# GpSimd's elementwise steps as one instruction each instead of two to four pieces, in an attention and feed-forward kernel

## The chip, the cores and the metric

The kernel runs on one core of one Trainium2 chip. The metric is device time in microseconds of one execution; the profile is one further execution with the hardware profiler on. Engines are named as the profile names them: PE is TensorE, DVE is VectorE, ACT is ScalarE, POOL is GpSimd, SP is SyncE (here the queue that issues the DMAs).

## What is computed

Four batches of eight heads, 768 rows, head width 64. Each row of Q and K gets a bucket from the signs of six projections; a score counts only where the buckets agree. After the softmax and the product with V, the heads of a row are joined to 512 numbers, which go through a feed-forward layer of width 2048 with the exact GELU.

```python
q_bits = (np.einsum('bhsd,dk->bhsk', q, proj) > 0)
k_bits = (np.einsum('bhsd,dk->bhsk', k, proj) > 0)
mask = q_bucket[:, :, :, None] == k_bucket[:, :, None, :]
scores = np.where(mask, scale * np.matmul(q, k.transpose(0, 1, 3, 2)), -1e9)
attn = exp(scores - max); attn = attn / (sum(attn) + 1e-09)
x = (attn @ v).transpose(0, 2, 1, 3).reshape(B * S, H * D)
h = x @ w_in
out = (0.5 * h * (1.0 + erf(h / sqrt(2)))) @ w_out
```

## The kernel before

**Numbers in two halves.** Most float32 products are made of float16 parts: a value is scaled by a power of two, rounded to a high half, and the rest becomes a low half. That takes a scaling (`affine`, one tensor input) and either one VectorE instruction of two SBUF inputs (scale and subtract in one) or, on GpSimd, a scaling in place and a subtraction (`subtract`, two tensor inputs). Such splits are made of Q and K of 24 heads (`head`, `add_low` at L625 on), of the two weight matrices (`weight_pair`), of V (`values_halves`) and of the attention weights (`unit`, `high` and `low` at L984 on). The first batch's heads keep plain float32 (`head_plain`), and the attention weights of some units are divided in place and turned by TensorE (`whole_turn`, L1031).

**A row block.** 32 heads of six blocks of 128 rows give 192 units. A unit is: scores on TensorE into one of two PSUM buffers `s` (L952 for plain heads, L954 and L955 for split ones); the row maxima on VectorE (L958, `rows<-s`); one or two 128x1 steps on GpSimd, VectorE or ScalarE (L963 and L438, `rows<-rows`); the exponential on ScalarE (L972), which sets the `s` buffer free for the next scores; a reciprocal (L981); the high half of the attention weights (L438 or L434, into `hl`, or into `wraw`, which serves as more of the same buffers after the weights are read); the low half on VectorE (L987); a DMA that transposes both halves (L994); and the product with V (L1084).

**A head** of the later batches: load (`raw`), largest value (L603), scale, high half `Q`, copies of it by DMA or an engine (`K<-Q`), the two low halves of Q and K (on GpSimd: `raw<-raw,hs` at L438 and `K<-raw,Q` at L459), the projections onto the six bits on TensorE (L668), their signs on ScalarE (L674), and the mask rows (`Q<-sign`).

**The feed-forward part** runs for 256 rows at a time: L1300 (hidden layer), L1310 (ScalarE takes it out of PSUM), L1338 (GELU), the high and low halves of the result (`g`, L438 and L1352) and L1382 (second product), L1412 (VectorE takes it out). TensorE works it in between the attention's units, and alone after the last of them.

**What sets the order.** A planner (`Plan.order`) plays all steps through with estimated costs and fixes each step's engine and each engine's order; the instructions are then written out in that order, and every engine works through its own in order, waiting on semaphores. The costs are numbers in `affine_cost`, `subtract_cost` and in the `on` tables of steps (2.8 for a low half on GpSimd). They hold for a step, however it is issued.

**The lines that the change touches.** `pieces` (L422) cuts a GpSimd step's tiles along the free dimension: an `affine` into pieces of at most 512 columns, a `subtract` into pieces of at most 256. So 768 columns are two pieces of 384 or three of 256, and 1,024 columns two of 512 or four of 256. Steps on VectorE and ScalarE are never cut, and GpSimd's steps of 512 columns or fewer in `affine` (`g`, the mask rows, the 128x1 steps) are one piece already.

Of the kernel before, what the change touches and what calls it, by code (L numbers as in the profile page):

```python
# [16 lines left out]
ALU = mybir.AluOpType  # L17
# [235 lines left out]
def tile_bucket_attention_moe(  # L253
# [94 lines left out]
    def buf(step):  # L348
# [32 lines left out]
        out=praw[:, NBIT:], in0=praw[:, :NBIT], scalar1=-1.0, scalar2=None, op0=ALU.mult  # L381
# [37 lines left out]
            top = add("DVE", 0.07, emit, key, [top], port=emit is inverse)  # L419
        return top  # L420

    def pieces(engine, most, *aps):  # L422

        whole, n = aps[0].shape[1], 1
        for size in aps[0].shape[1:]:
            n *= size
        count = -(-n // most) if engine == "Pool" else 1
        cuts = [whole * k // count for k in range(count + 1)]
        return [tuple(x[:, i:j] for x in aps) for i, j in zip(cuts, cuts[1:])]

    def affine(engine, out, in_, scale=1.0, bias=0.0):

        if engine == "ACT":
            nc.scalar.activation(out=out, in_=in_, func=AF.Copy, scale=scale, bias=bias)  # L434
        else:
            on = nc.vector if engine == "DVE" else nc.gpsimd
            for o, x in pieces(engine, 512, out, in_):
                on.tensor_scalar(out=o, in0=x, scalar1=scale, scalar2=bias, op0=ALU.mult, op1=ALU.add)  # L438

    def affine_cost(engine, n, pointer=False):  # L440
        base, rate, extra = {
# [13 lines left out]

    def subtract(engine, out, in0, in1):
        on = nc.vector if engine == "DVE" else nc.gpsimd
        for o, x, y in pieces(engine, 256, out, in0, in1):
            on.tensor_tensor(out=o, in0=x, in1=y, op=ALU.subtract)  # L459

    def subtract_cost(engine, n):
        return 0.14 + 1.042e-3 * n if engine == "DVE" else 0.2 + 2.2e-3 * n
# [4 lines left out]
    def everywhere(t, top, key):  # L467


        def diagonal():  # L470
            affine(dg.engine, buf(dg), ident, t[:, 0:1])

        def spread():
            nc.tensor.matmul(buf(pm)[:, :P], ones, buf(dg), start=True, stop=True)

        def biggest():
            nc.vector.tensor_reduce(out=t[:, 1:2], in_=buf(pm)[:, :P], axis=AX.X, op=ALU.max)

        dg = add(affine_on("DI", P, True), 0, diagonal, key, [top], takes="diag", port=True)
        pm = add("PE", 0.11, spread, key, [dg], takes="hp")  # L480
        free(dg, [pm])
        sc = add("DVE", 0.2, biggest, key, [pm])
        free(pm, [sc])
        return sc
# [105 lines left out]
    def head(b, h, i, key, clear, cl):  # L590
# [16 lines left out]
        def high():  # L607
            affine(hi.engine, aq, buf(raw), sc)

        def add_move(dst, src, rd, rs):  # L610
            box = []

            def move():
                out, in_ = sets[i][dst][rd], sets[i][src][rs]
                if box[0].engine == "SP":
                    nc.sync.dma_start(out=out, in_=in_)
                else:
                    affine(box[0].engine, out, in_)

            on = {  # L620
                "DVE": (0.27, PAR["NM_DVE"]), "ACT": (0.84, PAR["NM_ACT"]), "Pool": (0.9, PAR["NM_Pool"]),
                "SP": (0.45, PAR["NM_SP"]),
            }
            box.append(add(on, 0, move, key + PAR[f"DUP{cl}"], [hi], port=True))
            return box[0]  # L625

        def add_low(dst, rd, rs):
            box = []

            def low():  # L630
                out, a = sets[i][dst][rd], aq[rs]
                x = buf(raw)[rs]
                if box[0].engine == "DVE":
                    nc.vector.scalar_tensor_tensor(
                        out=out, in0=x, scalar=sc[rs], in1=a, op0=ALU.mult, op1=ALU.subtract
                    )
                else:
                    affine("Pool", x, x, sc[rs])
                    subtract("Pool", out, x, a)

            on = {"DVE": (1.04, PAR["NL_DVE"]), "Pool": (2.8, PAR["NL_Pool"])}
            box.append(add(on, 0, low, key + PAR[f"LOW{cl}"], [hi], port=True))
            return box[0]
# [57 lines left out]
    def weight_pair(name, srcs, dsts, inv, key, step):  # L701
# [76 lines left out]
        for f, dst in zip(fs, dsts):  # L778
            box = []

            def scaled(f=f, box=box):
                affine(
                    box[0].engine, buf(box[0]).rearrange("p (c f) -> p c f", c=n), f.bitcast(F32), t[:, 2:3]
                )

            def high(dst=dst, box=box):
                affine(box[1].engine, dst[:, 0], buf(box[0]).rearrange("p (c f) -> p c f", c=n))

            def low(dst=dst, box=box):
                subtract(  # L790
                    box[2].engine, dst[:, 1], buf(box[0]).rearrange("p (c f) -> p c f", c=n), dst[:, 0]
                )

            ws = add(affine_on("WS", 1024, True), 0, scaled, key + PAR["P" + name], [sc], takes="o", port=True)
            hi = add(affine_on("WH", 1024), 0, high, key + PAR["P" + name], [ws], port=True)
            lo = add(subtract_on("WL", 1024), 0, low, key + PAR["Q" + name], [hi], port=True)
            box += [ws, hi, lo]
            los.append(lo)
            splits[name][-1].append(ws)
            free(ws, [lo])  # L800
# [346 lines left out]
    whole = tuple((c, TC) for c in range(0, S, TC))  # L1147
# [26 lines left out]
    for n_pass, (b, chunks) in enumerate(passes):  # L1174
# [7 lines left out]
        for pos, h in enumerate(heads):  # L1182
            pr = h // 2
            if pos % 2 == 0:
                key, mms = t - PAR[f"V{cl}"], []
                whole = pos // 2 < WHOLE[n_pass]
# [6 lines left out]
            i = next((i for i in range(n_sets) if owner.get(i, ())[:2] == (b, h)), None)  # L1193
            kept = i is not None
            if not kept:
                i = min(range(n_sets), key=lambda i: (used.get(i, -1), i))
# [277 lines left out]
```

## Time and profile before

| | us |
|---|---|
| median of three runs | 916.1 (915.82 to 916.74) |
| the profiled execution | 916.96 |
| its span, first to last instruction | 915.1 |
| TensorE busy | 865.3 |
| VectorE busy | 677.9 |
| ScalarE busy | 648.7 |
| GpSimd busy | 484.9 in 745 instructions |

The profile is read as busy time of each engine, in the whole span and in stretches; as waits, each an idle time of an engine with the instruction that ended it; as groups of instructions with their durations; and as instructions in order of time. A duration on GpSimd or VectorE runs from the instruction's start to its end, so what it waits for with its operands ready, inside the instruction, makes it longer.

### The profile page before, as it was taken

What the parts mean: (1) busy time and instruction counts of PE and PEld (TensorE: products, weight loads), DVE (VectorE), ACT (ScalarE), POOL (GpSimd) and SP (SyncE); (2) the same over time, 40 slices, a digit from 0 to 9 for tenths busy, and PEclk for the clock granted to TensorE, in tenths of its full rate; (3) what the DMA queues carried; (4) which work ended last, traced back from release to release, by engine and by line L of the source; (5) the groups of instructions that cost most, each with busy time, mean ns of one, the idle gap of its engine ahead of it and who ended that gap; (6) DMA issues with size and microseconds to landing.
All of it is one profiled execution on the core that took longest, in us unless ns stands there. A gap on an engine that the chain in (4) does not pass through costs nothing. (4 is left out here: it accounts for less than half of the span.)

```text
span 915.1 us, 18464 instructions
## 1 busy us (share of the span) xinstructions
PE 865.3 (95%) x6893; PEld 574.4 (63%) x6893; DVE 677.9 (74%) x1441; ACT 648.7 (71%) x1090; POOL 484.9 (53%) x745
## 2 busy tenths in 40 slices
PE   8998999988999989999889999999999999999998
PEld 5665556654755746656647656656666667676763
DVE  5999997987997998888889988987878761212122
ACT  3798889987878787888888797887767653232221
POOL 2486769587758677776877477675723310000000
PEclk9999999999999999999999999999999999999999
DMA  9963362316777888776888876876775750000000
GB/s 256 248 181 111 92 188 70 93 31 122 166 159 149 152 184 172 139 151 151 132 166 172 184 167 139 162 142 127 116 122 116 127 117 1 24 2 24 1 24 24
DMA packets 282394, 112.17 MB, mean 123 GB/s; under 512 B 228800, under 2 KB 269888, under 8 KB 282304
## 3 DMA queue, kind: packets, MB, share of 16 engines
q1 hardware_dynamic: 282000, 110.98, 56.0%
q8 instruction: 54, 0.88, 0.4%
q14 instruction: 36, 0.29, 0.1%
q10 hardware_dynamic: 304, 0.00, 0.0%
HBM read 43.13 MB, written 6.29 MB: 54 GB/s over the span
## 5 line engine op out<-in xcount | busy, mean ns | idle before, releaser
L1300 PE MATMUL hp<-x,Win 128*128 128x256 f16 x2304 | 267.1, 273 | 2.8 <-DVE x L1112 2.4
L1382 PE MATMUL hp<-Wout,g 128*128 128x512 f16 x1152 | 261.6, 379 | 0.0
L1300 PEld LDWEIGHTS <-Win 128*128 128x128 f16 x2304 | 225.2, 98 | 42.4 <-issue 6.4
L1382 PEld LDWEIGHTS <-g 128*128 128x128 f16 x1152 | 109.9, 98 | 126.3 <-issue 4.4
L958 DVE TENSOR_REDUCE rows<-s 128x1 f32<-128x768 f32 x192 | 178.8, 945 | 7.4 <-PE s L955 5.7
L972 ACT ACTIVATE p<-s,rows 128x768 f32<-128x768 f32 x142 | 140.3, 988 | 22.4 <-POOL rows L438 10.5
L1310 ACT ACTIVATE h<-hp,ffs 128x512 f32<-128x512 f32 x96 | 65.5, 682 | 101.3 <-PE hp L1300 100.8
L954 PE MATMUL s<-Q 88*128 88x384 f16 x304 | 99.5, 327 | 13.9 <-ACT p L972 8.6
L955 PE MATMUL s<-K 128*128 128x384 f16 x304 | 99.4, 327 | 0.0
L459 POOL TENSOR_TENSOR K<-raw,Q 64x256 f16<-64x256 f32 x120 | 93.5, 805 | 3.2
L438 DVE TENSOR_SCALAR g<-h,ffs 128x512 f16<-128x512 f32 x30 | 15.0, 500 | 107.4 <-ACT h L1338 77.3
L1084 PE MATMUL hp<-pt,vhl 128*64 128x256 f16 x1296 | 77.6, 274 | 4.8 <-DVE o L1412 2.3
L987 DVE SCALAR_TENSOR_TENSOR hl<-p,rows,hl 128x768 f16<-128x768 f32 x66 | 72.2, 1096 | 13.4 <-POOL hl L438 11.2
L1084 PEld LDWEIGHTS <-vhl 128*64 128x64 f16 x1296 | 69.3, 110 | 14.6 <-issue 13.0
L1352 DVE SCALAR_TENSOR_TENSOR g<-h,ffs,g 128x512 f16<-128x512 f32 x96 | 74.8, 801 | 2.7 <-ACT g L434 0.6
L963 POOL TENSOR_SCALAR rows<-rows,hs 128x1 f32<-128x1 f32 x67 | 45.1, 674 | 57.5 <-DVE rows L958 52.8
L438 POOL TENSOR_SCALAR rows<-rows 128x1 f32<-128x1 f32 x109 | 49.3, 453 | 46.0 <-ACT p L972 26.9
L438 POOL TENSOR_SCALAR raw<-raw,hs 64x384 f32<-64x384 f32 x82 | 55.0, 675 | 20.3 <-ACT Q L434 8.2
L972 ACT ACTIVATE wraw<-s,rows 128x768 f32<-128x768 f32 x50 | 49.3, 987 | 11.2 <-POOL rows L438 3.9
L955 PEld LDWEIGHTS <-K 128*128 128x128 f16 x304 | 29.8, 98 | 37.6 <-issue 21.6
L438 DVE TENSOR_SCALAR rows<-rows 128x1 f32<-128x1 f32 x163 | 28.3, 179 | 29.6 <-ACT p L972 21.2
L438 POOL TENSOR_SCALAR hl<-p,rows 128x384 f16<-128x384 f32 x50 | 33.0, 672 | 30.0 <-DMA pt<-hl 20.8
(169 smaller groups left out, 1393.1 us busy)
## 6 DMA issues: line engine op xcount, KB each, us to landing
raw<-qk SPq DMA_DIRECT2D x27, 384.0 KB, 3.6
vraw<-v SPq DMA_DIRECT2D x24, 384.0 KB, 4.1
wraw<-w_in SPq DMA_DIRECT2D x16, 512.0 KB, 5.1
wraw<-w_out SPq DMA_DIRECT2D x16, 512.0 KB, 4.1
out<-o SPq DMA_DIRECT2D x11, 512.0 KB, 2.9
K<-Q SPq DMA_DIRECT2D x31, 96.0 KB, 2.2
Q<-Q SPq DMA_DIRECT2D x17, 96.0 KB, 2.7
pt<-hl SPq DMA_TRANSPOSE x97, 4.1
```

The lines of the kernel that those rows point to most:

```text
L438: on.tensor_scalar(out=o, in0=x, scalar1=scale, scalar2=bias, op0=ALU.mult, op1=ALU.add)
L459: on.tensor_tensor(out=o, in0=x, in1=y, op=ALU.subtract)
L954: nc.tensor.matmul(to, aq[kk, qs], ak[kk, n], start=True, stop=False)
L955: nc.tensor.matmul(to, bq[:, qs], bk[:, n], start=False, stop=True)
L958: nc.vector.tensor_reduce(out=nm, in_=both(sp), axis=AX.XY, op=ALU.max, negate=True)
L972: nc.scalar.activation(out=buf(ex).rearrange("p (b k) -> p b k", b=2), in_=both(sp), func=AF.Exp, scale=sc, bias=nb, accum_out=ssum,)
L987: nc.vector.scalar_tensor_tensor(out=buf(hi)[:, 1], in0=buf(ex), scalar=r, in1=buf(hi)[:, 0], op0=ALU.mult, op1=ALU.subtract,)
L1084: nc.tensor.matmul(pv[j * D : (j + 1) * D], buf(vh)[:, tv, kt, j * D : (j + 1) * D], buf(holds[j][0])[:, tp * KT + kt, :nt], start=kt == 0 ...
L1300: nc.tensor.matmul(buf(pair[0])[:, j * ch[1] : (j + 1) * ch[1]], win_hl[:, f0 // WB1, tw, pr, f0 % WB1 : f0 % WB1 + P], x[:, tx, pr, : ch[1]],
L1310: nc.scalar.activation(out=values_of()[:, 2 * fp : 2 * fp + 2, :nt], in_=buf(pair[0])[:, : 2 * nt].rearrange("p (j k) -> p j k", j=2), fun ...
L1352: nc.vector.scalar_tensor_tensor(out=gt[:, 1, s2, :nt], in0=h[:, s2, :nt], scalar=sg, in1=gt[:, 0, s2, :nt], op0=ALU.mult, op1=ALU.subtract,)
L1382: nc.tensor.matmul(buf(banks[u]).rearrange("p (c f) -> p c f", c=NWB), gt[:, tg, f, u * P : (u + 1) * P], wout_hl[:, :, tw, ft], start=ft ...
```

## The change

`pieces` is taken out, and `affine` and `subtract` issue each GpSimd step whole. The costs, the planner and its table stay.

```diff
-    def pieces(engine, most, *aps):
-
-        whole, n = aps[0].shape[1], 1
-        for size in aps[0].shape[1:]:
-            n *= size
-        count = -(-n // most) if engine == "Pool" else 1
-        cuts = [whole * k // count for k in range(count + 1)]
-        return [tuple(x[:, i:j] for x in aps) for i, j in zip(cuts, cuts[1:])]
-
     def affine(engine, out, in_, scale=1.0, bias=0.0):
 
         if engine == "ACT":
             nc.scalar.activation(out=out, in_=in_, func=AF.Copy, scale=scale, bias=bias)
         else:
             on = nc.vector if engine == "DVE" else nc.gpsimd
-            for o, x in pieces(engine, 512, out, in_):
-                on.tensor_scalar(out=o, in0=x, scalar1=scale, scalar2=bias, op0=ALU.mult, op1=ALU.add)
+            on.tensor_scalar(out=out, in0=in_, scalar1=scale, scalar2=bias, op0=ALU.mult, op1=ALU.add)
...
     def subtract(engine, out, in0, in1):
         on = nc.vector if engine == "DVE" else nc.gpsimd
-        for o, x, y in pieces(engine, 256, out, in0, in1):
-            on.tensor_tensor(out=o, in0=x, in1=y, op=ALU.subtract)
+        on.tensor_tensor(out=out, in0=in0, in1=in1, op=ALU.subtract)
```

On TensorE, VectorE, ScalarE and SyncE the same instructions stand in the same order; line numbers behind the cut are 10 or 11 lower, and some numbers at the ends of buffer names differ. GpSimd has 263 instructions fewer. Its rows for the low halves of one head (`K3_95`, at 345 to 358 us of the trace; `x2` and `x3` count equal rows in a row) read before:

```order
L438 TENSOR_SCALAR raw0_77<-raw0_77,hs_142 64x384 x2
L459 TENSOR_TENSOR K3_95<-raw0_77,Q3_94 64x256 x3
L438 TENSOR_SCALAR raw0_77<-raw0_77,hs_142 64x384 x2
L459 TENSOR_TENSOR K3_95<-raw0_77,Q3_94 64x256 x3
L438 TENSOR_SCALAR hl0_69<-p0_67,rows_96 128x384 x2
L963 TENSOR_SCALAR rows_96<-rows_96,hs_142 128x1
```

and after:

```order
L428 TENSOR_SCALAR raw0_77<-raw0_77,hs_142 64x768
L448 TENSOR_TENSOR K3_95<-raw0_77,Q3_94 64x768
L428 TENSOR_SCALAR raw0_77<-raw0_77,hs_142 64x768
L448 TENSOR_TENSOR K3_95<-raw0_77,Q3_94 64x768
L428 TENSOR_SCALAR hl0_69<-p0_67,rows_96 128x768
L952 TENSOR_SCALAR rows_96<-rows_96,hs_142 128x1
```

Each row of pieces has become one instruction of 768 columns; nothing has moved past anything else.

GpSimd's rows for the weights `Wout` and its scaled copies `o` (149 to 160 us of the trace) read before:

```order
L438 TENSOR_SCALAR Wout_99<-o1_86 128x512 x2
L459 TENSOR_TENSOR Wout_99<-o1_86,Wout_99 128x256 x4
L438 TENSOR_SCALAR o0_85<-Wout_99,tiny_97 128x512 x2
L438 TENSOR_SCALAR o1_86<-Wout_99,tiny_97 128x512 x2
L438 TENSOR_SCALAR rows_96<-rows_96 128x1
```

and after:

```order
L428 TENSOR_SCALAR Wout_99<-o1_86 128x1024
L448 TENSOR_TENSOR Wout_99<-o1_86,Wout_99 128x1024
L428 TENSOR_SCALAR o0_85<-Wout_99,tiny_97 128x1024
L428 TENSOR_SCALAR o1_86<-Wout_99,tiny_97 128x1024
L428 TENSOR_SCALAR rows_96<-rows_96 128x1
```

The same holds here with 1,024 columns. Where the pieces were tracked one by one, a reader of the first columns alone waited for the first piece alone: TensorE's first transposes of a divided block (L1031) and its first projections of a head (L668) had a wait of their own for a later piece, and now wait once, for the whole step.

## Rows read from the trace of the kernel before

**Rows 1.** The page, busy us of each engine (share of the span) and instructions.
```profile
PE 865.3 (95%) x6893; PEld 574.4 (63%) x6893; DVE 677.9 (74%) x1441; ACT 648.7 (71%) x1090; POOL 484.9 (53%) x745
```

**Rows 2.** Windows: start:end, us, busy us (instructions) by engine, clock, DMA.
```profile
0.00:200.00 200.00, 182.12 (x1470) 123.82 (x1471) 173.56 (x442) 166.00 (x305) 134.30 (x229) 0.99 0.51 143
200.00:700.00 500.00, 472.30 (x3886) 309.24 (x3887) 429.55 (x872) 404.80 (x678) 336.59 (x495) 1.00 0.74 149
```

**Rows 3.** Waits of TensorE: us in total, times, longest us.
```profile
PE s L954 <- ACT p L972: 8.6, 18, 1.7
PE hp L668 <- POOL K L459: 6.7, 9, 1.6
...
PE s L952 <- ACT p L972: 3.6, 8, 1.1
```

**Rows 4.** GpSimd's groups by form: count | busy us, mean ns | idle before.
```profile
L459 POOL TENSOR_TENSOR K<-raw,Q 64x256 f16<-64x256 f32 x120 | 93.5, 805 | 3.2
L438 POOL TENSOR_SCALAR raw<-raw,hs 64x384 f32<-64x384 f32 x82 | 55.0, 675 | 20.3 <-ACT Q L434 8.2 <-DVE Q L438 5.5 <-issue 2.6
...
L438 POOL TENSOR_SCALAR x<-raw,hs 128x384 f16<-128x384 f32 x2 | 1.7, 869 | 2.4 <-PE s L952 2.4
```

**Rows 5.** Tiles on GpSimd: ns minimum/median/maximum, first and last start us.
```profile
L459 POOL TENSOR_TENSOR K<-raw,Q x120: 662/669/1396, 89.9 to 659.4; 64x256 f16<-64x256 f32 x120
...
L438 POOL TENSOR_SCALAR p<-p,rows x22: 583/606/1127, 28.4 to 191.4; 128x384 f32<-128x384 f32 x22
...
L438 POOL TENSOR_SCALAR o<-Wout,tiny x10: 687/692/1368, 147.0 to 183.4; 128x512 f32<-128x512 f32 x10
...
L438 POOL TENSOR_SCALAR rows<-rows x109: 191/268/1467, 22.0 to 739.3; 128x1 f32<-128x1 f32 x109
```

**Rows 6.** Timeline, 657 to 661 us: start us, us, engine and instruction, count.
```profile
657.11 1.81 DVE L1352 SCALAR_TENSOR_TENSOR g<-h,ffs,g 128x512 f16<-128x512 f32 x2
657.15 3.64 POOL L459 TENSOR_TENSOR K<-raw,Q 64x256 f16<-64x256 f32 x3
658.85 1.42 DVE L987 SCALAR_TENSOR_TENSOR hl<-p,rows,hl 128x768 f16<-128x768 f32 x1
660.19 1.42 DVE L987 SCALAR_TENSOR_TENSOR hl<-wraw,rows,hl 128x768 f16<-128x768 f32 x1
...
660.84 0.48 PE L668 MATMUL hp<-K,hash 128*32 128x384 f16 x5 [1.00 <-POOL K L459]
```

**Rows 7.** Timeline, 352 to 355 us.
```profile
352.22 2.64 POOL L459 TENSOR_TENSOR K<-raw,Q 64x256 f16<-64x256 f32 x3
...
352.94 1.39 DVE L987 SCALAR_TENSOR_TENSOR wraw<-wraw,rows,wraw 128x768 f16<-128x768 f32 x1
...
354.91 0.48 PE L668 MATMUL hp<-K,hash 128*32 128x384 f16 x5 [1.00 <-POOL K L459]
```

**Rows 8.** Tiles on VectorE, columns as in the fifth group.
```profile
L987 DVE SCALAR_TENSOR_TENSOR hl<-p,rows,hl x66: 992/1017/1491, 205.2 to 740.6; 128x768 f16<-128x768 f32 x66
...
L1352 DVE SCALAR_TENSOR_TENSOR g<-h,ffs,g x96: 730/745/1190, 169.8 to 901.3; 128x512 f16<-128x512 f32 x96
```

**Rows 9.** VectorE's groups of the same two, columns as in the fourth group.
```profile
L1352 DVE SCALAR_TENSOR_TENSOR g<-h,ffs,g 128x512 f16<-128x512 f32 x96 | 74.8, 801 | 2.7 <-ACT g L434 0.6
L987 DVE SCALAR_TENSOR_TENSOR hl<-p,rows,hl 128x768 f16<-128x768 f32 x66 | 72.2, 1096 | 13.4 <-POOL hl L438 11.2 <-ACT hl L434 2.0
```

**Rows 10.** Waits of VectorE and ScalarE for GpSimd, columns as in the third group.
```profile
DVE hl L987 <- POOL hl L438: 18.4, 17, 2.8
...
ACT rows L434 <- POOL rows L963: 14.0, 14, 2.6
```

**Rows 11.** Timeline, 319 to 322 us.
```profile
319.58 0.69 ACT L1310 ACTIVATE h<-hp,ffs 128x512 f32<-128x512 f32 x1
...
320.34 0.99 ACT L972 ACTIVATE p<-s,rows 128x768 f32<-128x768 f32 x1
...
321.47 0.32 PE L954 MATMUL s<-Q 88*128 88x384 f16 x1 [0.90 <-ACT p L972]
```

## Prediction

> **What bounds the kernel now.** I read the busy shares first, then the stretches, then who waits for whom, then single places in time. TensorE is busy 95% of the span [rows 1]; its work does not change, so the end can move only through its idle time, 915.1 - 865.3 = 49.8 us. The stretch after the attention can gain nothing: GpSimd's last small step starts at 739.3 [rows 5], and behind that TensorE runs the feed-forward part alone. In the stretches before it (0 to 200 and 200 to 700) TensorE is busy 91% and 94%, VectorE 87% and 86%, GpSimd 67% [rows 2]. So TensorE sets the time, VectorE is the fuller of the two engines that the change touches, and GpSimd has slack on average. What matters is where TensorE stands still. Two causes stand out [rows 3]: it waits for the exponentials (first and last of three such rows shown; 18 + 7 + 8 = 33 waits, against 192 row blocks), and at L668 it waits 9 times, 6.7 us in all, for the GpSimd subtraction at L459. The second cause is a step that the change rewrites.
>
> How such a wait comes about is seen at 657 us [rows 6]: GpSimd starts its three pieces at 657.15 and needs 3.64 us, while VectorE runs four instructions with two SBUF inputs in the same time. The two alternate: a piece, a VectorE instruction, a piece. VectorE's L987 takes 1.42 us there where its median is 1.017 [rows 8], GpSimd's pieces up to 1.396 where the median is 0.669 [rows 5], and TensorE waits 1.00 us for the last piece. Whichever engine holds what the two share keeps it to the end of its instruction, and the other's instruction is long by the rest.
>
> **The change part by part.** Order: every engine keeps its order; only GpSimd's neighbouring pieces become one row (the listings ahead). No DMA, queue or buffer moves, so the price lies in durations and in who waits on whom.
>
> *One-input steps.* 13 groups of 278 pieces (largest and smallest in [rows 4]) become 139 instructions. 384 columns take at least 583 ns, 512 columns 687 [rows 5], that is 0.81 ns a column; 768 columns come to 583 + 384 x 0.81 = 895 ns. Two pieces take 2 x 583 = 1,166, so 0.27 us go per step, 38 us of GpSimd's time.
>
> *Subtractions.* 41 steps of three pieces (120 of the 123 are one row of [rows 4]) and 14 of four. Only one size is on record, 256 columns at 662 ns at least [rows 5], so the whole one is bounded: with no fixed part 3 x 662 = 1.99 us, no gain; with the fixed part that one-input steps extrapolate to (583 - 384 x 0.81 = 272 ns) 272 + 3 x 390 = 1.44 us. I take 191 ns, the shortest 128x1 step [rows 5], the nearest thing to a bare fixed part: 191 + 3 x 471 = 1.60 us. That is 0.39 us less per undisturbed step. Besides, 40 of them are busy 93.5 us [rows 4], 2.34 each, 0.35 over 1.99: VectorE cutting in between pieces. It can't any more.
> The Trainium skill, GPSIMD Engine Reference, section 3.1, gives 4,497 ns for a two-input step of 2,048 columns; an estimate through that and 256 columns is 1.75 us for 768. No run here shows it. By it the sum below would be smaller by about 0.5 us.
>
> *At L668.* Place by place I set 1.60 us in for the pieces. At 352.22 [rows 7] the three pieces take 2.64 us; whole, and started 0.27 earlier, the step ends at 353.6 instead of 354.9, which removes the 1.00 us wait; VectorE's L987, which starts at 352.94, waits to 353.6 and ends as late as now. At 657.15 GpSimd waits about 0.55 us for a VectorE instruction under way, then ends near 659.3 instead of 660.8, and the wait of 1.00 goes almost whole. Over the nine waits I keep 0.7 of 6.7 us: **6.0 us** of idle time go at first order. Not all is kept, since the next wait on the path is for an exponential, and ScalarE may be what is late there. At 321 us the exponential starts at 320.34, right where the instruction in front of it ends (319.58 + 0.69) [rows 11]; a faster GpSimd ahead of it would give nothing. I keep half: **-3.0 us**.
>
> *VectorE.* It gains and loses. Gain: it waits 17 times, 18.4 us, for GpSimd's first half of a split (`hl`) [rows 10]; each is 0.27 earlier, 4.6 us. Loss: the time that VectorE instructions now lose behind GpSimd is mean less median times count: L987 66 x (1096 - 1017) = 5.2 us in its largest group, L1352 96 x (801 - 745) = 5.4 [rows 8, 9]; these two are half of VectorE's time in instructions of that kind, so some 20 us in all (an estimate). By the GpSimd instruction under way, about half of it lies behind subtractions, a quarter behind one-input pairs, a quarter behind steps that stay as they are. Behind a whole instruction the rest to wait for grows from 0.67 to 1.6 and from 0.58 to 0.9; yet one step can stop VectorE once, not three times as at 657. Bounds: 0 (GpSimd holds the shared part for less time in all) and +16 us (20 x (0.5 x 1.6/0.67 + 0.25 x 0.9/0.58 + 0.25) = 36, none saved). I take +9, so net +4.4 us on VectorE. One row block in six leaves TensorE waiting for its exponential now, and lateness uses up the slack of as many more; with a third reaching the end: **+1.5 us**.
>
> *The first 200 us.* The whole division at L438 (`p<-p,rows`, 11 steps) lets TensorE's first transposes start 0.3 us later, since they waited for the first piece alone; against that the weight steps of 1,024 columns end 0.3 to 0.6 us earlier each. Bounds +1 and -2; I take **-0.6**, nearer the weight steps because there are 30 of them.
>
> Sum: -3.0 + 1.5 - 0.6 = **-2.1 us**. The profiled execution took 916.96 us (span 915.1 and 1.9 around it), so 914.9; it lies 0.9 over the median of the runs, and the same step from 916.1 gives **914.0 us**.
>
> **Rivals.** *The longer holds decide.* VectorE, not GpSimd, is at 86% in the long stretch, and a whole subtraction can stop it 1.4 us at a stroke in front of the row maxima and reciprocals that every exponential needs. At its upper bound, +16 us with the shorter pairs hidden elsewhere, half reaches TensorE (+8), less 3 kept at L668: **921 us**; at the middle of that, 919. It decides from where VectorE's net loss is over some 12 us, that is from L987 at a mean near 1.2 us. For it: ScalarE waits 14.0 us for one kind of small step alone whose inputs VectorE makes [rows 10], so the chain has little room. Against: at 352 and 657 the VectorE chain ends 0.0 and 0.3 us later, while GpSimd ends 1.3 and 1.5 earlier.
> The Trainium skill states this as a rule: SBUF — State Buffer, "Who interferes with whom", says that the shared port pair is held for a whole instruction, first come, and the other blocks. The trace agrees (1.42 against 1.017 us); what it can't say is which of the two engines the path needs first.
>
> *Nothing reaches the end.* The exponentials pace TensorE in three rows of waits against one; what L668 gives is lost at the next score block, as at 321 us. Then only the remainders stand: **916 us**. For it: ScalarE is 81% full in that stretch [rows 2]. Against: scores start earlier when TensorE does, so its chain moves with it.
>
> *The steps get no cheaper*: if the fixed part were zero, 1.99 us for a subtraction, L668 would still gain from the missing interruptions and VectorE would lose the more; that ends in the first rival's range.
>
> **How the numbers follow.** A measurement of this kernel can tell some 0.2%, 1.8 us, from no change: faster is under 914.3, slower over 917.9. The forecast, 909.5 to 914.3, has 0.38; its low end is all 6.0 us kept and VectorE's loss at zero. Nothing reaching the end, 914.3 to 917.9, has 0.28, and the longer holds, 917.9 to 922, have 0.34. The range reaches from 909.5 to 921, leaving out a tail of the gain and the worst of the loss, some 2 in 10. The three cases are the three chances; the forecast is only a little ahead, since two effects of 3 to 8 us with opposite signs are set against each other.
>
> **What would show it.** GpSimd: 482 instructions instead of 745, one-input steps near 0.9 us and subtractions between 1.44 and 1.99, busy near 410 us instead of 485. TensorE at L668: under 1.5 us of waits for L459. VectorE: L987 at a mean of 1.1 to 1.2 us, busy 680 to 690. If L668's waits go and TensorE's waits for exponentials grow by as much, the half that I kept was wrong; if L987's mean is over 1.2 and its waits stand in front of late exponentials, the first rival holds. If subtractions take more than 1.99, the whole working falls.

## The result and the profile after

| | before | after |
|---|---|---|
| median of the runs, us | 916.42 (915.82 to 917.70) | 895.28 (893.87 to 898.14) |
| ratio to before, 95% interval | | 0.9771 (0.9745 to 0.9798) |
| profiled execution, span | 916.96, 915.1 | 895.55, 893.8 |
| TensorE busy, and idle in the span | 865.3, 49.8 | 865.9, 27.9 |

The kernel became 2.3% faster, 21 us where 2.1 were forecast, and 895.3 lies below the range. The line numbers of after are 10 or 11 lower (L668 is L657, L459 is L448, L438 is L428, L954 is L943, L987 is L976). The page's first line and the two stretches of [rows 1, 2], after:

```profile
PE 865.9 (97%) x6893; PEld 577.4 (65%) x6893; DVE 675.6 (76%) x1441; ACT 648.0 (72%) x1090; POOL 399.0 (45%) x482
```
```profile
0.00:200.00 200.00, 186.85 (x1459) 127.43 (x1460) 173.43 (x439) 164.25 (x302) 111.35 (x140) 0.97 0.51 143
200.00:700.00 500.00, 489.14 (x4100) 324.39 (x4099) 442.52 (x904) 420.89 (x706) 284.24 (x337) 1.00 0.78 154
```

TensorE's work is the same and 21.9 us of its idle time are gone. TensorE runs the same 6,893 products in the same order in both kernels, so the count begun is a clock of progress: after 200 us it is 1,459 against 1,470, not ahead at all, and in the next 500 us it is 4,100 against 3,886. Counted product by product in the two traces, after is 3.3 us behind at 165 us, 3 us ahead at 270, 10 at 368, 19 at 462 and 21.4 from 655 us to the end. The gain is made between 200 and 655 us, a little at every head.

TensorE's waits after (us in total, times, longest), beside [rows 3]:

```profile
PE s L943 <- ACT p L961: 6.8, 14, 0.9
PE s L941 <- ACT p L961: 3.3, 5, 1.4
PE s L943 <- ACT wraw L961: 1.4, 2, 1.1
```

No wait of L657 for the subtraction is left in the trace. The three waits for exponentials were 16.8 us before (8.6 and 3.6 of them in [rows 3], the third here):

```profile
PE s L954 <- ACT wraw L972: 4.6, 7, 1.6
```

They have not grown by what L668 gave up; they fell to 11.5.

GpSimd's two groups of the low halves (count | busy us, mean ns | idle before) and tiles (minimum/median/maximum ns, first and last start), beside [rows 4, 5]:

```profile
L448 POOL TENSOR_TENSOR K<-raw,Q 64x768 f16<-64x768 f32 x40 | 69.3, 1732 | 3.3
```
```profile
L448 POOL TENSOR_TENSOR K<-raw,Q x40: 1637/1642/2228, 88.0 to 635.9; 64x768 f16<-64x768 f32 x40
L428 POOL TENSOR_SCALAR raw<-raw,hs x41: 895/912/1679, 58.5 to 634.9; 64x768 f32<-64x768 f32 x41
...
L428 POOL TENSOR_SCALAR rows<-rows x109: 192/267/1934, 21.6 to 718.0; 128x1 f32<-128x1 f32 x109
```

A subtraction takes 1.64 us (three pieces left alone: 1.92 from the first start to the last end, 2.0 as a sum of durations), a scaling 0.91 (two pieces: 1.17 as a sum), and GpSimd's last small step starts at 718.0 instead of 739.3: the 21.3 us are there when the attention ends.

VectorE's two groups and the waits for GpSimd, beside [rows 8 to 10]:

```profile
L976 DVE SCALAR_TENSOR_TENSOR hl<-p,rows,hl 128x768 f16<-128x768 f32 x66 | 73.3, 1112 | 4.0 <-ACT hl L425 2.3 <-POOL hl L428 1.5
L1341 DVE SCALAR_TENSOR_TENSOR g<-h,ffs,g 128x512 f16<-128x512 f32 x96 | 73.1, 784 | 2.7 <-ACT g L425 0.6
```
```profile
DVE hl L976 <- POOL hl L428: 6.0, 5, 2.4
ACT rows L425 <- POOL rows L952: 5.6, 8, 1.7
```

The place of [rows 7] is at 342 us now (start, us, engine and instruction, count), and two lines from the low half ahead of it:

```profile
339.20 1.64 POOL L448 TENSOR_TENSOR K<-raw,Q 64x768 f16<-64x768 f32 x1
...
339.70 1.96 DVE L976 SCALAR_TENSOR_TENSOR hl<-p,rows,hl 128x768 f16<-128x768 f32 x1
...
342.52 1.65 POOL L448 TENSOR_TENSOR K<-raw,Q 64x768 f16<-64x768 f32 x1
...
344.14 0.58 PE L657 MATMUL hp<-K,hash 128*32 128x384 f16 x8
```

The subtraction takes 1.65 us instead of 2.64, and the projection starts as it ends. The second line is the price: VectorE's L976 starts inside a whole subtraction, waits for its end and takes 1.96 us. The same instruction before:

```profile
348.42 1.22 DVE L987 SCALAR_TENSOR_TENSOR hl<-p,rows,hl 128x768 f16<-128x768 f32 x1
```

### The profile page after: what moved, and what is told of

It is laid out like the page before. It is cut to its first block, busy times and chain, and to the rows that moved or that the text cites. A ratio compares the mean times of both kernels' runs of the same rounds, so it can differ in the third digit from the quotient of the medians.

```text
span 893.8 us, 18191 instructions
## 1 busy us (share of the span) xinstructions
PE 865.9 (97%) x6893; PEld 577.4 (65%) x6893; DVE 675.6 (76%) x1441; ACT 648.0 (72%) x1090; POOL 399.0 (45%) x482
## 5 line engine op out<-in xcount | busy, mean ns | idle before, releaser
L943 PE MATMUL s<-Q 88*128 88x384 f16 x304 | 99.4, 327 | 8.8 <-ACT p L961 6.8
L428 DVE TENSOR_SCALAR g<-h,ffs 128x512 f16<-128x512 f32 x30 | 15.1, 503 | 108.5 <-ACT h L1327 78.5
L976 DVE SCALAR_TENSOR_TENSOR hl<-p,rows,hl 128x768 f16<-128x768 f32 x66 | 73.3, 1112 | 4.0 <-ACT hl L425 2.3
L1073 PEld LDWEIGHTS <-vhl 128*64 128x64 f16 x1296 | 69.0, 110 | 10.7 <-issue 9.2
L1341 DVE SCALAR_TENSOR_TENSOR g<-h,ffs,g 128x512 f16<-128x512 f32 x96 | 73.1, 784 | 2.7 <-ACT g L425 0.6
L428 POOL TENSOR_SCALAR rows<-rows 128x1 f32<-128x1 f32 x109 | 43.6, 400 | 67.1 <-ACT p L961 42.7
L952 POOL TENSOR_SCALAR rows<-rows,hs 128x1 f32<-128x1 f32 x67 | 43.4, 648 | 65.5 <-DVE rows L947 60.7
L448 POOL TENSOR_TENSOR K<-raw,Q 64x768 f16<-64x768 f32 x40 | 69.3, 1732 | 3.3
L428 POOL TENSOR_SCALAR raw<-raw,hs 64x768 f32<-64x768 f32 x41 | 45.2, 1103 | 19.8 <-ACT Q L425 8.5
L941 PE MATMUL s<-K,Q 76*128 76x384 f32 x112 | 44.6, 531 | 3.3 <-ACT p L961 3.1
L1020 PE MATMUL hp<-ident,p 128*128 128x128 f32 x276 | 43.1, 291 | 4.5 <-DVE tiny L466 1.7
```

The costliest lines, as they stand in the source:

```text
L428: on.tensor_scalar(out=out, in0=in_, scalar1=scale, scalar2=bias, op0=ALU.mult, op1=ALU.add)
L448: on.tensor_tensor(out=out, in0=in0, in1=in1, op=ALU.subtract)
L943: nc.tensor.matmul(to, aq[kk, qs], ak[kk, n], start=True, stop=False)
L976: nc.vector.scalar_tensor_tensor(out=buf(hi)[:, 1], in0=buf(ex), scalar=r, in1=buf(hi)[:, 0], op0=ALU.mult, op1=ALU.subtract,)
L1073: nc.tensor.matmul(pv[j * D : (j + 1) * D], buf(vh)[:, tv, kt, j * D : (j + 1) * D], buf(holds[j][0])[:, tp * KT + kt, :nt], start=kt == 0 ...
L1341: nc.vector.scalar_tensor_tensor(out=gt[:, 1, s2, :nt], in0=h[:, s2, :nt], scalar=sg, in1=gt[:, 0, s2, :nt], op0=ALU.mult, op1=ALU.subtract,)
```

## Experiments

The expectations name theories by letters. *Speed* (A): GpSimd does less work, and its time counts in proportion, wherever it is; A' says the same of how late its results come. *Interruptions* (B): what counts is that VectorE no longer cuts in between pieces. *Low halves* (C for the waits at L668 alone, D in the later runs for all that hangs on these steps): only the 41 low halves of Q and K (`add_low`: a scaling of `raw`, then the subtraction into `K`) count, by the time from the scaling's start to the subtraction's end. All kernels compute the whole result; the fillers are small writes to a spare tile that nothing reads. "Low half" is the mean of those 41 times in the trace; "wait" is TensorE's at the projection (L668) that ends with the subtraction (us, times); "idle" is span less TensorE's busy time in the profiled execution, which for e5 took 901.4 us, 7 more than the median. Line numbers of the runs with fillers are a few off again.

| run | us | ratio (95%) | low half, us | wait | idle |
|---|---|---|---|---|---|
| before | 914.6 to 916.6 | 1 | 3.80 | 6.7, 9 | 49.8 |
| after | 895.3 | 0.977 (0.975 to 0.980) | 2.92 | none | 27.9 |
| e1_affine_whole | 901.0 | 0.984 (0.981 to 0.988) | 3.37 | 1.4, 3 | 32.3 |
| e2_subtract_whole | 897.0 | 0.981 (0.977 to 0.985) | 3.18 | 2.5, 2 | 36.1 |
| e3_low_whole | 894.3 | 0.978 (0.974 to 0.981) | 2.84 | 0.2, 1 | 29.5 |
| e6_all_but_low | 906.1 | 0.989 (0.985 to 0.994) | 3.77 | 3.9, 6 | 39.5 |
| e4_finer | 990.9 | 1.083 (1.079 to 1.087) | 5.25 | 27.8, 20 | 89.0 |
| e11_low_finer | 964.6 | 1.054 (1.051 to 1.058) | 5.26 | 26.0, 21 | 70.5 |
| e5_fill_after | 894.6 | 0.977 (0.972 to 0.982) | 2.95 | none | 34.3 |
| e7_fill_front | 904.1 | 0.988 (0.983 to 0.992) | 3.17 + 0.36 | 2.2, 3 | 37.8 |
| e8_fill_behind | 903.2 | 0.987 (0.983 to 0.991) | 2.82 | 1.5, 3 | 34.9 |
| e9_low_late | 898.8 | 0.981 (0.978 to 0.985) | 3.23 + 0.36 | 2.0, 3 | 33.6 |
| e9b_low_late_twice | 923.2 | 1.007 (1.004 to 1.011) | 3.74 + 0.57 | 8.3, 5 | 50.2 |
| e10_rest_late | 895.2 | 0.979 (0.976 to 0.982) | 2.87 | none | 30.2 |

"+" is the filler in front of the scaling, the median time from its start to the scaling's. Rows marked "none" have no such wait in the profile's list. In e7 two waits of 1.4 us together, and in e8 all three, are put down to a filler that starts as the low half's subtraction ends; they are counted here.

**Each half of the change alone, and the reverse of it.** Edits against before: e1 and e2 leave one of the two helpers cutting; e4 cuts the steps of 768 columns finer.

```diff
 e1: -            for o, x in pieces(engine, 512, out, in_):
 e1: +            for o, x in pieces(engine, 2048, out, in_):
 e2: -        for o, x, y in pieces(engine, 256, out, in0, in1):
 e2: +        for o, x, y in pieces(engine, 2048, out, in0, in1):
 e4: +            for o, x in pieces(engine, 192 if in_.shape[1] == 768 else 512, out, in_):
 e4: +        for o, x, y in pieces(engine, 128 if in0.shape[1] == 768 else 256, out, in0, in1):
```

> One-input steps whole (139 instructions instead of 278), subtractions still in pieces of 256. Theory A (GpSimd's own time: the 21 us come in proportion to the 86 us of GpSimd busy time that went, some 38 of it here): near 907 us. Theory B (VectorE cutting in between the pieces, which is worst in the three-piece subtractions): 911 to 914. Theory C (only the low halves of Q and K in front of L668): 909 to 914, the L668 waits cut by a third.

> Subtractions whole, one-input steps still in two pieces. Theory A (in proportion to GpSimd's time, 45 of 86 us): near 905 us. Theory B (cut-ins): 898 to 902, since 41 + 14 subtractions hold most of the cut-ins. Theory C (low halves before L668): 898 to 905, with the L668 waits under 1 us.

> Twice as many pieces in steps of 768 columns: four of 192 and six of 128 (1,024 columns: scalings four of 256, subtractions as before). Theory A: some 85 to 95 us more of GpSimd's time, so 935 to 940 us. Theory B: as many VectorE instructions cut in, only at more places: 918 to 925. Theory C: 920 to 930 with L668 waits doubled or more.

Either half alone brings most of the gain, 14 and 18 us of 21, so they don't add: what the second one saves is mostly no longer on the path. Finer pieces make GpSimd's busy time 83.6 us longer (568.5 against 484.9) and the span 72.4 us (987.5 against 915.1), though GpSimd is busy only 58% of it; e3 (below) and after differ by 48 us of GpSimd's time and by nothing at the end. Of the 72.4 us, 39.2 are idle time of TensorE and 33.2 are busy time, at a mean granted clock of 0.965 instead of 0.996. e1 also speaks against the interruptions as such: its subtractions are still in pieces and still cut into (mean 760 ns where the shortest takes 661), and two thirds of the gain is there.

**Time put back without cutting.** Tiny writes are added to the kernel after: two behind each whole scaling of more than 512 columns and three behind each such subtraction (e5), or five and nine, in front (e7) or behind (e8).

```diff
+    spare = const.tile([P, 4, 8], BF16, tag="spare", name="spare")
+    def filler(engine, out, count):
...
+            for k in range(count):
+                nc.gpsimd.memset(spare[:, k % 4], 0.0)
```

> Everything whole as in the changed kernel, and behind each formerly cut step two or three small memsets of a spare tile on GpSimd, which give back about the time that the pieces cost (0.25 to 0.4 us a step, some 50 to 60 us in all) without reading SBUF and without being in front of the step's own reader. Theory A: 908 to 916 us, most of the gain gone. Theory B: 895 to 899, the gain stays. Theory C: 896 to 902.

> Everything whole, and in front of each formerly cut step small memsets of a spare tile (five before a scaling, nine before a subtraction, each adding some 67 ns by the trace of the run with fillers behind: 0.33 and 0.60 us, 80 us in all, about what the pieces cost). The step's reader gets it as late as with pieces, but nothing can cut into the step. Theory A' (lateness of GpSimd's results): 908 to 918 us. Theory B (the cutting in itself, that is VectorE and GpSimd taking turns): 894 to 900.

> The same 1,190 memsets, all behind the step (for a low half of Q or K behind its subtraction, none between scaling and subtraction). The step's reader is served as early as in the changed kernel, GpSimd's next step as late as with pieces. Theory A' (lateness): 900 to 910, less than with the fillers in front, since only what queues behind is late. Theory B: 894 to 900, as in front.

e5 puts 29.6 us of work back into GpSimd and loses nothing (two of its fillers do stand in front of the low half's subtraction, which puts 0.17 us between the two instead of 0.08). e7 and e8 add some 63 us, so that GpSimd is busy 459 and 455 us, and lose 8 to 9 us. So 30 us of queue time cost nothing and 63 us cost 40% of the gain: not a price in proportion. In e8 the low halves are as short as after (2.82 us); what is late is whatever stands behind a step on GpSimd, the next low half too, and the projection waits three times, 1.5 us in all. E8's group of the fillers, TensorE's wait at the projection, and ScalarE's wait for 128x1 steps of GpSimd:

```profile
L430 POOL MEMSET spare<- 128x8 bf16 x1190 | 63.9, 110 | 3.6
```
```profile
PE hp L670 <- POOL spare L430: 1.5, 3, 0.7
```
```profile
ACT rows L435 <- POOL rows L965: 10.9, 13, 2.1
```

The last was 14.0 before [rows 10] and 5.6 after. Which of the two waits carries e8's loss is open.

**Which steps.** e3 issues only the low halves whole (against before), e6 everything but them.

```diff
-    def affine(engine, out, in_, scale=1.0, bias=0.0):
+    def affine(engine, out, in_, scale=1.0, bias=0.0, most=512):
...
-                    affine("Pool", x, x, sc[rs])
-                    subtract("Pool", out, x, a)
+                    affine("Pool", x, x, sc[rs], most=2048)
+                    subtract("Pool", out, x, a, most=2048)
```

> Only the low halves of Q and K are issued whole (scaling and subtraction of add_low), all other steps in pieces. Theory C (the way to L668): 895 to 900, nearly all of the gain. Theory A' or B: 899 to 907, a share by the number of steps (82 of 194) with the subtractions among them, as the run with subtractions whole gave 897.

> The complement: everything whole except the low halves of Q and K. Theory C: 911 to 916, nearly no gain. Theory A' or B: 900 to 908; since the two single-kind runs gave 14 and 18 us of 20 together, the halves should again add up to more than the whole.

e3 has the whole gain, with 82 whole steps and 622 GpSimd instructions. Its busy line, and its low-half groups:

```profile
PE 864.9 (97%) x6893; PEld 577.0 (65%) x6893; DVE 675.2 (75%) x1441; ACT 647.7 (72%) x1090; POOL 447.2 (50%) x622
```
```profile
L459 POOL TENSOR_TENSOR K<-raw,Q 64x768 f16<-64x768 f32 x40 | 66.8, 1671 | 3.3
...
L438 POOL TENSOR_SCALAR raw<-raw,hs 64x768 f32<-64x768 f32 x41 | 44.5, 1086 | 17.8 <-ACT Q L434 8.3 <-DVE Q L438 4.4 <-issue 2.6
```

GpSimd is busy 447.2 us, only 37.7 of the 85.9 us less, and the time is that of after. Set beside e6 this is a table of two by two: both cut 916, only the low halves whole 894, only the rest whole 906, both whole 895. With the low halves whole the rest is worth nothing (-1 us, inside the spread); with the low halves cut the rest is worth about 9 us (906.1 against 914.7 in the same set of runs). e6 has less GpSimd time than e3 (437.1 us) and is 12 us slower, which ends the theory of speed in proportion. TensorE's waits in e6:

```profile
PE s L954 <- ACT p L972: 5.8, 11, 2.1
PE s L954 <- ACT wraw L972: 4.3, 5, 1.3
PE hp L668 <- POOL K L459: 3.9, 6, 1.0
```

**The low halves alone, later.** Against after, e9 puts the fillers of e7 in front of the low halves only (5 before the scaling, 9 before the subtraction), e9b twice as many, e10 in front of all other formerly cut steps. e11 issues the rest whole, as e6, and cuts the low halves as finely as e4.

```diff
 e9:  +                    filler(5)
                           affine("Pool", x, x, sc[rs])
 e9:  +                    filler(9)
                           subtract("Pool", out, x, a)
```

> The changed kernel, everything whole, with memsets in front of the 41 low halves of Q and K alone (five before the scaling, nine before the subtraction, about 0.9 us a step and 38 us in all). Theory D (the 41 steps sit in the chain that decides, and their lateness alone is what the pieces cost): 906 to 914 us, the waits at L668 back at 4 to 8 us. Theory B (the cutting in between pieces): 894 to 899.

> The same with twice the memsets (some 1.9 us a step, 76 us in all). Theory D: 940 to 970, each further microsecond of the chain in full and more, on the way to the 991 us of the finer pieces. Theory B: 898 to 905.

> The complement: the same memsets in front of all formerly cut steps except the low halves of Q and K (98 scalings with five, 14 subtractions with nine; some 41 us). Theory D: 894 to 899, nothing or little is lost, as the run with only the low halves whole gave 894.3. Theory A' (lateness of any GpSimd step counts alike): 903 to 908.

> Only the low halves of Q and K in finer pieces (four of 192 columns, six of 128), everything else whole. Theory D: 960 to 985 us, most of what the finer pieces cost over all (991). Theory A': 925 to 940, a share by GpSimd's time. Theory B: 915 to 935.

e10 and e9 are the first pair: the same kind of filler, about as many (616 and 574), costs nothing in front of the rest (895.2) and 3.5 us in front of the low halves. That difference alone shows little: the intervals of e9, e10 and after overlap, and in e9 VectorE is busy longer as well (688.7 us against 678.5 in e10 and 675.6 after), because more of its instructions start inside a low half's subtraction (20 of them lose 16.3 us there, 9 lose 4.8 after). Doubled (e9b) the fillers cost 28 us, 24 of them over e9, with VectorE's busy time as in e9 (689.3). This decides: e9b has as many fillers as e7 and e8 (1,148 and 1,190), which cost 8 to 9 us when spread over all steps, and 28 when all stand in front of the low halves. e9b's low-half group, fillers, and TensorE's wait for the subtraction:

```profile
L454 POOL TENSOR_TENSOR K<-raw,Q 64x768 f16<-64x768 f32 x40 | 71.3, 1781 | 1.6
L426 POOL MEMSET spare<- 128x8 bf16 x1148 | 53.8, 110 | 2.3
```
```profile
PE hp L665 <- POOL K L454: 8.3, 5, 3.0
```

e9b ends the theory that only the interruptions count: every step in it is whole, and it is slower than the kernel that cuts all of them. Cutting matters because it makes the low halves longer (3.80 us where 3.14 is the shortest in pieces), and length from any other source does the same. The finer low halves of e11 go on along the line; its busy line, its wait and its long stretch:

```profile
PE 893.7 (93%) x6893; PEld 587.0 (61%) x6893; DVE 675.7 (70%) x1441; ACT 650.1 (67%) x1090; POOL 488.4 (51%) x810
```
```profile
PE hp L668 <- POOL K L459: 26.0, 21, 2.9
```
```profile
200.00:700.00 500.00, 452.62 (x3579) 290.30 (x3578) 393.85 (x808) 382.44 (x637) 340.16 (x584) 0.96 0.68 138
```

From e6 to e11 only the low halves change, by 1.49 us each, 41 x 1.49 = 61 us; the span grows by 61.3. That equality is half a coincidence: TensorE's idle time grows by 31.0 us, and its busy time by 30.3 at a lower granted clock (last part).

**Against the expectations.** The forecasts of size were often missed. e1 came out under the ranges of all three theories, e2 a microsecond or more under them, and e4 50 us over the highest. e6 (906.1) lies in the range of A' and B and under that of C. e9 (898.8) lies in the range of B and under the 906 to 914 of D, and e9b (923.2) between B and D; the lateness of a low half cost less than D said. e7 (904.1) lies between A' and B. e3 and e5 are within 1 us of the low ends of C and of B, e8 in the range of A', and e10 and e11 in those of D alone.

In sum: up to a low half of about 3 us the time is flat at 894 to 895; from there it rises, by 2 to 9 us at 3.2 to 3.5, 11 to 21 at 3.8, 28 at 3.74 + 0.57. The flat part holds where GpSimd has at most some 35 us of fillers. The two ends at 3.8 (e6 and before), and the losses of e8 at 2.82 and e7 at 3.17, show that the length alone is not the whole rule: how much other GpSimd work stands around it shifts the point. How the loss reaches the end, by TensorE's wait at the projection or by the small steps queued behind on GpSimd, no run separates. The waits speak for the first. ScalarE's wait for 128x1 steps of GpSimd doesn't follow the time: it is 11.5 us in e2 (897.0), 8.6 in e6 (906.1) and 8.2 in e9b (923.2). TensorE's idle time before L668 does for the most part: 0.1 us after, 0.5 in e3, 5.3 in e6, 7.8 before, 10.7 in e9b, 26.9 in e11 and 29.4 in e4; e2, at 4.4, is the exception. ScalarE's wait in e6 and in e9b:

```profile
ACT rows L434 <- POOL rows L963: 8.6, 10, 2.5
```
```profile
ACT rows L431 <- POOL rows L960: 8.2, 8, 2.1
```

No version is clearly better than the change itself: e3 (894.3), e5 (894.6), e10 (895.2) and after (895.3) lie within each other's spread.

## Why the prediction was wrong

**What held.** 482 instructions as said. Scalings: 895 ns predicted, median 912. Subtractions: 1.60 us taken between 1.44 and 1.99, median 1.642. The estimate from the figure of the Trainium skill (GPSIMD Engine Reference, section 3.1) was 1.75 us; the runs lie nearer the value from rows. GpSimd's busy time: about 410 predicted, 399.0. L657's waits: under 1.5 us predicted, none listed. The place at 352 us went as worked out for GpSimd and TensorE (1.65 us, projection without a wait); VectorE's L987, which was to wait inside the subtraction there, starts after it and takes 1.01 us.

**The step that failed: "I keep half", -3.0 us.** It was right that the 6.0 us at L668 would go, and wrong that half of them would turn up again as waits for exponentials. The prediction had named what would show the half wrong, waits for exponentials that grow; they fell, by 5.3 us. By lines (TensorE's idle time before its products in the groups of the trace), L668 lost 7.8 us, L954 5.1 (13.9 to 8.8), L1084 4.0, L560 2.7, and L1031, L1300 and L952 together 2.3: 21.9, the whole gain, of which 7.8 were visible as L668's. e3 shows that all of this hangs on the low halves: with them alone made whole, the idle time at L954 falls to 7.8 and at L1031 to 4.3, though nothing at those steps changed. Against these 7.8 us the gain is 2.7 times as large (21 us), and against the 6.0 us of the prediction 3.5 times, where it took 0.5: the term was -3.0 us and measured some -21.

Why it multiplies is argued and not shown. TensorE works in order, so a projection that waits holds up the scores and products behind it, and with them the maxima and exponentials of the next row blocks. GpSimd works in order too, so a low half that takes 3.80 us instead of 2.92 delays the 128x1 steps behind it, on which exponentials wait: ScalarE's wait for those steps fell from 14.0 to 5.6 us with the change, and to 7.3 in e3, whose small steps are as before. But it is 8.6 in e6 too, whose low halves are cut and which is 12 us slower than e3, so this second way can't be the main one by that wait. The prediction moved the nine places forward one by one and let nothing else move; at 321 us it saw an exponential that followed right on another ScalarE instruction and took ScalarE for the next limit. But that place, ScalarE's instructions with it, comes 8.2 us earlier in after: ScalarE was no limit of its own there.

**"GpSimd has slack on average" [rows 2]** was true and misleading. The code has a number that would have said so: the planner's cost of a low half is 2.8 us. The step took 3.80 in the trace of before, one microsecond over its plan, 41 times, in an order that was laid out with 2.8; after it takes 2.92, and below about 3 us the runs are flat. That the plan's 2.8 is why the bend lies there is argued, since no run changed the plan, and an overrun by itself does not tell which steps count: the plan has 0.88 us for a scaling of 768 columns (`affine_cost`), in e3 the 98 scalings other than those of the low halves are still in two pieces, those of `hl` 0.71 us a piece, and nothing is lost. The prediction compared durations of pieces, and never the step with its planned cost.

**VectorE, +1.5 us: 0.** The mechanism is there. VectorE's L976 takes 1.96 us at 339.70, inside a subtraction. That agrees with the rule of the Trainium skill (SBUF — State Buffer, "Who interferes with whom") that the engine which comes first has the shared ports for its whole instruction. The size was wrong: I took +9 us of longer holds out of bounds 0 and +16. Summed over VectorE's instructions of two inputs with a scaling (`SCALAR_TENSOR_TENSOR`, grouped by names and shape) that take over 80 ns more than the shortest of their group, the time lost is 20.7 us in 70 instructions before and 19.2 in 39 after: longer stops, and fewer. L976's mean rose by 16 ns only (1096 to 1112), and L1341's fell (801 to 784). The value at the lower bound, "one step can stop VectorE once, not three times", was the right one. VectorE's busy time fell to 675.6 us, under the 680 to 690 that were to show the loss. The gain beside it was larger than the 4.6 us: VectorE's waits for first halves fell from 18.4 to 6.0.

**First 200 us, -0.6: some 2 us the other way.** TensorE's idle time there fell by 4.7 us (17.9 to 13.2), but its busy time rose by as much, 182.1 to 186.9 us, for 11 products fewer (1,459 against 1,470), at a granted clock of 0.97 instead of 0.99; at 195 us after is 2.3 us behind. The clock was no term of the sum, and the result lies outside its bounds of +1 and -2. That the change brought the lower clock is not shown: in those 200 us it is 0.99 in e2 and e6, 0.98 in e10 and 0.96 in e3.

**The rivals.** "The longer holds decide" needed L987 at 1.2 us and fell at 1.11. "Nothing reaches the end" took it that the next score block loses what L668 gives, as the kept half did in part, and fell with it. What neither the forecast nor a rival had was a case in which a wait's removal is worth more than the wait; the range's low end, 909.5, was "all 6.0 us kept", as if that were the most that could be had.

## What to carry to other kernels

Where engines work through fixed orders, a wait of TensorE that recurs at each head or tile need not be worth its own length. Here, in the four runs with most idle time at the projection (before, e9b, e11 and e4, 7.8 to 29.4 us), the span is longer than that of after by 2.6 to 3.2 times that idle time, the clock's part included. So work such a wait out at half and at three times its length, and let the range reach both. Compare each step's measured duration with the cost that the plan was laid out with, since a step over its plan delays everything queued behind it on its own engine too, even where that engine is 67% busy; then find out which of the overruns matter. And look at which of an engine's steps stand in the deciding chain: here whole issue of 41 low halves brought all of the gain with 37.7 of the 85.9 us saved, and the other 48 us were worth nothing on top of it (some 9 us alone).

## What the runs showed of the hardware

**Cost of cutting on GpSimd.** A subtraction of 768 columns takes 1.64 us whole (median after), 1.92 in three pieces of 256 left alone (shortest before, first start to last end), and 2.35 in six pieces of 128 left alone (shortest in e11; with interruptions 3.02 on average). In rows of two or more, a write of 128x8 numbers takes 47 to 67 ns (e9b: 53.8 us for 1,148; e5: 29.6 us for 443).

**The granted clock.** In after it falls between 90 and 100 us and again between 120 and 140, where before has the full clock (before falls to 0.83 between 10 and 20 us, where after doesn't). The two windows from 80 us on after, and the second of them before:

```profile
80.00:90.00 10.00, 8.59 (x69) 5.93 (x66) 9.89 (x23) 9.01 (x21) 2.82 (x3) 1.00 0.66 194
90.00:100.00 10.00, 9.92 (x36) 5.95 (x37) 7.73 (x21) 7.64 (x13) 5.63 (x7) 0.66 0.26 76
```
```profile
90.00:100.00 10.00, 7.63 (x40) 4.49 (x39) 9.14 (x23) 9.33 (x16) 7.99 (x15) 1.00 0.43 123
```

TensorE had stood still for 1.41 us up to 89.97; 0.66 is a mean of the lower level (1.2 GHz) and the full one (2.4 GHz), and eight products of L941 take 4.46 us there that took 2.92 before. Before had stood still for 1.08 us at the same place and kept the full clock. In e11, with more and longer stops, the clock over the long stretch is 0.96, and TensorE's busy time rises from 863.4 to 893.7 us against e6 for the same products: half of that run's longer span. A wait can so cost its own time and slower products after it, and a window that looks busier may hold less work.
